# Talking-heads attention and two feed-forward layers on one core: the second head mix with its weights stationary on 64x32 tiles, transposes on VectorE, and attn @ v on 64x64 tiles

## The chip, the cores and the metric

The kernel runs on 1 core of a Trainium2 chip. The metric is the device time of one execution in microseconds (us), the median of several runs; lower is better.

## What is computed

```python
scores = scale * np.matmul(q, k.transpose(0, 1, 3, 2))            # 4 batches, 12 heads, 448 x 448, head size 64
scores = np.einsum('bhij,hg->bgij', scores, w_pre)                # first mix over heads
scores = scores - np.max(scores, axis=-1, keepdims=True)
attn = np.exp(scores)
attn = attn / (np.sum(attn, axis=-1, keepdims=True) + 1e-09)
attn = np.einsum('bhij,hg->bgij', attn, w_post)                   # second mix over heads
x = np.matmul(attn, v)                                            # to 1792 tokens x 768
h = x @ w_in; g = s * np.maximum(h, 0) ** 2 + b; x = g @ w_out    # layer 1, 768 -> 2048 -> 768
h = x @ w_in2; g = h * np.cos(h); out = g @ w_out2                # layer 2
```

All inputs and the output are fp32.

## The kernel before, in words

The first part (`attention`, lines 199 to 481) computes the attention, the second (`mlp`, line 500 on) the two layers. The change touches the attention alone, apart from three tables of numbers that set the order.

**Tiling of the attention.** The 448 query rows of a batch are cut into 4 blocks (`BLOCKS`) of 120 or 110 rows, and a block into tiles of 10 rows (`R`): 45 tiles a batch, 180 in all. Tiles are worked on in pairs, 90 of them. Steps of the program, by the name of the tile that each writes:

- `heads` (line 288) loads q and k of two heads by DMA (`raw`, in batch 0 `at` serves as the room for it), turns them on TensorE (`tk`, `tq`, line 306, 48 steps of 4 transposes) and copies the result out of PSUM to `kt` and `qt`.
- `scores` (line 324) multiplies q and k of two heads for one block, on the two 64-row halves of the array (`sps`, line 336, 96 steps of 2 matmuls of 448 columns). Two copies bring the result out of PSUM into `s`, two DMAs per step (line 352) from there into `m`, in which a partition is a pair of row and head.
- `mix` (line 387) is the first mix, for a pair of tiles: 4 matmuls of 448 columns, on the four 64x64 quarters of the array, into two PSUM tiles `p` (line 393). VectorE takes the row maxima (`rmax`, line 400, `st`), ScalarE the exponentials with their sums (`expo`, line 406, `e`), VectorE adds 1e-9 and inverts (lines 412 and 413), GpSimd multiplies w_post by the inverse sums (`weigh`, line 415, `w`).
- `mixt` (line 421) is the second mix, again for a pair of tiles: 16 matmuls, 4 chunks of 112 keys by 2 halves of a tile's rows by 2 tiles. Here `e` (60 x 112) is the stationary operand and the weights `w` are streamed, 60 columns, so that the result `a` comes out with keys on the partitions:

```python
for c in range(4):
    for y in range(2):
        for z in range(2):
            nc.tensor.matmul(out=ha[z].tile[...][:, c, :, y * G:(y + 1) * G], lhsT=he.tile[64 * z:64 * z + K, y, c * CH:(c + 1) * CH],
                             rhs=hw2.tile[64 * z:64 * z + K, y], start=True, stop=True, tile_position=(64 * z, 0))
```

- `keep` (line 441) copies each `a` (112 x 480) into `at`, on ScalarE or VectorE.
- `prod` at line 458 is attn @ v, once per half batch and 4 heads (24 steps): 16 matmuls `vps` (line 464) of 112 x 64 weights from `v` and 230 or 220 columns from `at`, 2 side by side in the array's columns; 2 copies to `xo`, one DMA to `x` in HBM (line 475).

**What sets the order.** Every step is given to a planner (`Plan`, line 38) with a position (`pos`, a due time), the engines that may do it and a cost on each. `Plan.run` keeps a clock per engine, and lets each engine take the ready step with the smallest position; the program is then emitted in that order, and each engine executes its own instructions in it. A step marked `EV` (the copies out of PSUM) goes to ScalarE or VectorE, whichever the planner finds free. `STEP`, `LEAD`, `OFF`, `PRO`, `VW`, `W1` to `W3`, `AVP`, `AVL`, `TOK`, `WT0` and `TAIL` make the positions.

**Rings.** A step that writes a tile waits until the tile's ring has a free place. In PSUM, 8 banks: `ps` has 2 places (for `tk`, `tq`, `sps` and `vps`; a `sps` step takes both, each of the others one), `pa` 2 (both for one `mixt`), `pp` 4 (two for one `mix`). `at` has 2 places, a half batch each; `m` has 2, a block each.

The `mlp` part loads weights, splits each into two parts on ScalarE, VectorE and GpSimd, and runs `hidden` (`h`, line 704) and `output` (`o`, lines 767 and 797); its first steps are placed among the last ones of the attention.

Of the kernel before, what the change touches and what calls it, by code (L numbers as in the profile page):

```python
# [22 lines left out]
CH = 112  # L23
TOKENS = (512, 512, 256, 512)
# [170 lines left out]
STEP = 2374.9  # L195
# [3 lines left out]
def attention(pl, tc, q, k, v, w_pre, w_post, cst, x, mid, left, right, psl, psr):  # L199
# [6 lines left out]
    NG = H // 2  # L206

# [80 lines left out]
    def heads(what, b, g, p):  # L288
# [4 lines left out]
        def raw(new=False):  # L293
            if b == 0:
                i = g * 8 * D
                return at_all[:CH, int(what == "q")].rearrange("p c h w -> p (c h w)")[:, i:i + 8 * D].rearrange("p (z h d) -> p z h d", h=2, z=4)
# [19 lines left out]
    v_all = v_p.tile([CH, 3, 4, 4, D], F32, name="v")  # L316

    def values(b, c, p):
        hv = vh[b, c] = pl.hold(f"v{c}")
# [4 lines left out]
    def scores(n, g, p):
# [19 lines left out]
        first_e = pl.add(p + 800, EV, (430.0, 535.0), lambda e: evac(e, 0), [a], take=[hs], use=hp[:1])  # L344
        ev = [first_e, pl.add(p + 850, EV, (430.0, 535.0), lambda e: evac(e, 1), [a], use=hp[1:], behind=[first_e])]
# [35 lines left out]
    for i in range(NTL // 2):  # L381
# [13 lines left out]
        a = pl.add(p - OFF[0] * STEP, "pe", 840, mix, [d for n in ms for d in m_done[n]] + [c1, m_zero], take=hp, use=[mh[n] for n in ms])  # L395
# [3 lines left out]
        for y in range(2):  # L399
# [4 lines left out]
            m = pl.add(p - (OFF[1] - .1 * y) * STEP, "dve", 560, rmax, [a] + got[:1], take=[] if y else [hst])  # L404
# [474 lines left out]
```

## Time and profile before

| | us |
|---|---|
| median of 3 runs (1410.46 to 1412.24) | 1411.2 |
| the profiled execution, its own time | 1410.2 |
| its span, first to last instruction | 1408.4 |

The profile is of that one execution; the 1.8 us between its time and its span lie around the instructions. Busy time of an engine over the span: TensorE's matmuls (PE) 98%, its weight loads (PEld) 78%, VectorE (DVE) 78%, ScalarE (ACT) 47%, GpSimd (POOL) 31%. A busy time is the length of all records laid over one another, and the records of matmuls overlap, so that a PE that shows as busy has not always all it could do. The rows that matter follow below, each view with its columns.

### The profile page before, as it was taken

The page shows a single profiled execution, that of the slowest core. Times are in us where ns is not written, and L with a number is a line of the kernel's source. Part 1 is how long each engine was busy: PE and PEld are TensorE (multiplying, and loading weights), DVE is VectorE, ACT ScalarE, POOL GpSimd, SP SyncE. Part 2 cuts the span into 40 slices and gives each one's busy share as a digit, 9 for nine tenths or more (in the row PEclk, how much of TensorE's full clock was granted, in tenths as well). Part 3 has the DMA queues.
Part 4 walks back from the last instruction along what each step waited for, and adds up shares of the span by engine and source line. Part 5 has one row for each costly group of instructions (what it writes and reads, how often), then busy time and mean ns, then how long its engine had stood idle before and what let it go on. Part 6 is the DMA issues. An engine that isn't in the chain of part 4 may idle for free.

```text
span 1408.4 us, 25444 instructions
## 1 busy us (share of the span) xinstructions
PE 1383.4 (98%) x9753; PEld 1103.6 (78%) x9753; DVE 1095.8 (78%) x2052; ACT 665.8 (47%) x1385; POOL 429.7 (31%) x415
## 2 busy tenths in 40 slices
PE   7999999999999899999999999999999999999999
PEld 3466565666666688888888888889999999899998
DVE  3566666576577688889887787898799999998975
ACT  1575465465467454323232232466645545445442
POOL 2010000010012443423333243235554444554531
PEclk6899999999999999999999999999999999999999
DMA  6645456444444422221121212112121111211103
GB/s 132 183 129 146 143 138 156 138 130 140 139 148 141 142 68 68 68 67 58 54 71 34 67 47 65 36 34 68 46 68 46 57 57 45 69 45 57 56 35 123
DMA packets 120605, 123.80 MB, mean 88 GB/s; under 512 B 49476, under 2 KB 108324, under 8 KB 120484
## 3 DMA queue, kind: packets, MB, share of 16 engines
q1 hardware_dynamic: 117880, 120.43, 29.6%
q10 hardware_dynamic: 2604, 1.75, 0.5%
q8 instruction: 77, 1.26, 0.4%
q14 instruction: 44, 0.36, 0.1%
HBM read 72.43 MB, written 11.01 MB: 59 GB/s over the span
## 4 chain that ended last, share of the span: by engine, by line
PE 96%; DVE 1%; DMA 1%; ACT 1%; SPq 0%; issue 0%; POOL 0%; DVEq 0%; POOLq 0%
PE h L704 33%; PE o L797 17%; PE o L767 16%; PE a L427 11%; PE sps L336 7%; PE p L393 6%; PE vps L464 5%; PE tq L306 1%; PE tk L306 1%; DMA m<-s 0%; SPq L229 0%; DMA at<-in_q_dram 0%; DMA m<-x 0%; DVE s L235 0%; DVE x L680 0%
## 5 line engine op out<-in xcount | busy, mean ns | idle before, releaser
L652 POOL TENSOR_TENSOR cm<-ca,wh 128x384 f32<-128x384 f32 x128 | 160.8, 1258 | 363.3 <-ACT wh L646 362.6
L704 PE MATMUL h<-m,wh 128*128 128x512 f32 x672 | 217.0, 392 | 0.0
L704 PE MATMUL h<-x,wh 128*128 128x512 f32 (+1 forms) x768 | 192.0, 341 | 5.2 <-DVE x L680 3.8
L427 PEld LDWEIGHTS a<-w,e 60*112 60x112 f32 x2880 | 153.6, 176 | 50.8 <-issue 29.3
L654 POOL TENSOR_TENSOR wl<-cm,ce 128x384 fp32r<-128x384 f32 x128 | 147.5, 1154 | 93.4 <-DVE ce L650 87.3
L427 PE MATMUL a<-w,e 60*112 60x60 f32 x2880 | 161.6, 261 | 3.7 <-POOL w L417 3.5
L417 POOL TENSOR_TENSOR w<-wq,st 128x120 f32<-128x120 f32 x90 | 35.5, 396 | 396.5 <-DVE st L413 306.9
L704 PEld LDWEIGHTS h<-x,wh 128*128 128x128 f32 x768 | 133.0, 190 | 22.5 <-DVE x L680 4.8
L704 PE MATMUL h<-m,wl 128*128 128x512 f32 x384 | 150.6, 392 | 0.0
L704 PEld LDWEIGHTS h<-m,wh 128*128 128x128 f32 x672 | 125.4, 188 | 25.8 <-issue 0.7
L767 PE MATMUL o<-gl,wh 128*128 128x512 f32 (+1 forms) x384 | 139.6, 364 | 0.0
L767 PE MATMUL o<-gh,wl 128*128 128x512 f32 (+1 forms) x384 | 139.6, 364 | 0.0
L409 ACT ACTIVATE e<-p,st 128x448 f32<-128x448 f32 x180 | 113.2, 630 | 55.4 <-DVE st L403 41.6
L767 PE MATMUL o<-gh,wh 128*128 128x512 f32 (+1 forms) x384 | 139.3, 363 | 0.0
L704 PE MATMUL h<-x,wl 128*128 128x512 f32 (+1 forms) x384 | 130.9, 341 | 0.0
L403 DVE TENSOR_REDUCE st<-p 128x1 f32<-128x448 f32 x180 | 109.5, 618 | 21.7 <-PE p L393 19.4
L336 PE MATMUL sps<-kt,qt 64*110 64x448 f32 (+1 forms) x384 | 109.3, 613 | 6.7 <-DVE s L235 5.3
L797 PE MATMUL o<-wh,gl 128*128 128x384 f32 x448 | 114.3, 335 | 0.0
L797 PE MATMUL o<-wh,gh 128*128 128x384 f32 x448 | 114.2, 335 | 0.0
L797 PE MATMUL o<-wl,gh 128*128 128x384 f32 x448 | 114.2, 335 | 0.0
L744 POOL TENSOR_TENSOR tb<-ta,tb 128x512 f32<-128x512 f32 (+1 forms) x64 | 79.0, 1234 | 114.3 <-ACT tb L742 109.4
L806 DVE TENSOR_TENSOR acc<-acc,o 128x384 f32<-128x384 f32 x196 | 99.7, 545 | 14.3 <-PE o L797 14.2
(86 smaller groups left out, 2616.6 us busy)
## 6 DMA issues: line engine op xcount, KB each, us to landing
m<-s SPq DMA_DIRECT2D x144, 192.5 KB
raw<-in_moe_w_in_dram SPq DMA_DIRECT2D x64, 384.0 KB
raw<-in_moe_w_out_dram SPq DMA_DIRECT2D x64, 384.0 KB
m<-s SPq DMA_DIRECT2D x42, 210.0 KB
v<-in_v_dram SPq DMA_DIRECT2D x12, 448.0 KB
out_dram<-acc SPq DMA_DIRECT2D x13, 384.0 KB
raw<-in_k_dram SPq DMA_DIRECT2D x18, 224.0 KB
raw<-in_q_dram SPq DMA_DIRECT2D x18, 224.0 KB
```

The source lines that it names most:

```text
L336: nc.tensor.matmul(out=hp[z].tile, lhsT=hq.tile[64 * z:64 * z + 64, i0:i0 + rows], rhs=hk.tile[64 * z:64 * z + 64], start=True, stop=True, ...
L393: nc.tensor.matmul(out=hp[y].tile[64 * z:64 * z + 64], lhsT=wp[64 * y:64 * y + (K if y else 64)], rhs=src[64 * y:64 * y + (K if y else 64) ...
L403: nc.vector.tensor_reduce(out=hst.tile[:, 0, y:y + 1], in_=hp[y].tile, axis=AX, op=ALU.max, negate=True)
L409: nc.scalar.activation(out=he.tile[:, y], in_=hp[y].tile, func=AF.Exp, bias=hst.tile[:, 0, y:y + 1], accum_out=hst.tile[:, 1, y:y + 1])
L427: nc.tensor.matmul(out=ha[z].tile.rearrange("p (c g r) -> p c g r", c=4, g=H)[:, c, :, y * G:(y + 1) * G], lhsT=he.tile[64 * z:64 * z + K, ...
L652: a = pl.add(p0 + 6 * dp, "pool", 1050, lambda hm=hm, ha=ha, flat=flat: nc.gpsimd.tensor_tensor(out=hm.tile, in0=ha.tile.bitcast(F32), in1 ...
L654: got.append(pl.add(p0 + 7 * dp, "pool", 1050, lambda hm=hm, he=he, flat=flat: nc.gpsimd.tensor_tensor(out=flat(1), in0=hm.tile, in1=he.ti ...
L704: nc.tensor.matmul(out=hp.tile, lhsT=w, rhs=cols(z_, j, k)[:, 0], start=(k == 0 and y == 0), stop=(k == KD - 1 and y == 2))
L744: a = pl.add(p + 7 * dp, "pool", n * 2.4 + 100, lambda h1=h1, h2=h2: nc.gpsimd.tensor_tensor(out=h2.tile, in0=h1.tile, in1=h2.tile, op=ALU ...
L767: nc.tensor.matmul(out=hp.tile, lhsT=w, rhs=x, start=(c == 0 and y == 0), stop=(c == 1 and y == 2))
L797: nc.tensor.matmul(out=hp[e].tile, lhsT=x, rhs=w[:, e * HD:(e + 1) * HD], start=(c == 0 and y == 0), stop=(c == 1 and y == 2))
L806: got.append(pl.add(p, "dve", 470, lambda e=e, hp=hp, view=view: nc.vector.tensor_tensor(out=view(), in0=view(), in1=hp[e].tile, op=ALU.ad ...
```

## The change

The second mix is turned round. The weights `w` (60 x 32, 30 columns of them weights and 2 zeros) are now the stationary operand, and `e` is streamed, 224 columns: 7 runs of 32 keys, every second run of 32. Each of the 16 matmuls of a pair of tiles sits on one of eight 64x32 tiles of the array (2 in the rows, 4 in the columns), and the result `a` has 4 groups of 32 partitions (two halves of the heads by two runs of keys), with the keys along the free axis, 448 in all per tile. `keep` now is a VectorE transpose of 32x32 squares out of PSUM into `at` (2 per pair, each 128 x 448), and always on VectorE. With keys on 64 partitions and two halves of the heads above one another, attn @ v becomes 28 matmuls on the four 64x64 quarters, 7 steps along the keys, in two PSUM tiles, so that it takes both places of `ps`; each matmul streams runs of 5 elements of `at`, one run every 32. `v` is loaded in 24 DMAs of 64 partitions with pieces of 64 elements, in place of 12 with pieces of 256. The copies out of `vps` are 4 of 110 or 120 elements in place of 2 of 220 or 240, `xo` is written in runs, and `kt` and `qt` too are written in order and read in steps from PSUM. The planner's costs and positions are set anew.

```diff
-    wq = one.tile([128, H, G], F32, name="wq")
+    wq = one.tile([128, 64], F32, name="wq")
...
-            copy(e, ht.tile.rearrange("p (w z) -> p z w", z=4) if what == "q" else ht.tile.rearrange("p (z w) -> p z w", z=4), hp.tile)
-        t_done[what, b, g] = pl.add(p + 600, EV, (430.0, 535.0), evac, [a], use=[hp])
+            copy(e, ht.tile.rearrange("p (w z) -> p w z", z=4), hp.tile.rearrange("p z w -> p w z"))
+        t_done[what, b, g] = pl.add(p + 600, EV, (600.0, 680.0), evac, [a], use=[hp])
...
-    v_all = v_p.tile([CH, 3, 4, 4, D], F32, name="v")
+    v_all = v_p.tile([128, 3, 2 * KB, D], F32, name="v")
...
+        v_done[b, c] = got = []
+        for z in range(2):
+            got.append(dma(p, lambda z=z: v_all[64 * z:64 * z + 64, c], lambda z=z: v[b, GH * z + 2 * c:GH * z + 2 * c + 2].rearrange("h (k p) d -> p (h k) d", p=64),
+                           64 * 2 * KB * D * 4, take=[] if z else [hv], behind=got[:1] + m_done[0][-1:], rate=200.0))
...
-            for c in range(4):
-                for y in range(2):
-                    for z in range(2):
-                        nc.tensor.matmul(out=ha[z].tile.rearrange("p (c g r) -> p c g r", c=4, g=H)[:, c, :, y * G:(y + 1) * G], lhsT=he.tile[64 * z:64 * z + K, y, c * CH:(c + 1) * CH],
-                                         rhs=hw2.tile[64 * z:64 * z + K, y], start=True, stop=True, tile_position=(64 * z, 0))
+                h.tile = ps_a.tile([128, 512], F32, tag="a", name="a")[:, :2 * KB * 32]
+            for y in range(2):
+                for u in range(2):
+                    for c in range(2):
+                        for z in range(2):
+                            o = 64 * u + 32 * c
+                            nc.tensor.matmul(out=ha[z].tile[o:o + 32].rearrange("p (y k w) -> p y k w", y=2, w=32)[:, y], lhsT=hw2.tile[64 * z:64 * z + K, y, 32 * u:32 * u + 32],
+                                             rhs=he.tile[64 * z:64 * z + K, y].rearrange("p (k c w) -> p k c w", c=2, w=32)[:, :, c], start=True, stop=True, tile_position=(64 * z, o))
...
-            def keep(e, h=ha[z], slot=slot, col=col):
-                copy(e, at_all[:CH, slot].rearrange("p c h w -> p (c h) w")[:, :, col:col + R], h.tile.rearrange("p (c r) -> p c r", r=R))
-            kept[half].append(pl.add(p + 1000 + 100 * z, EV, (500.0, 600.0), keep, [a] + kept[half][:1], take=[hb] if new else [], use=ha[z:z + 1]))
+            def keep(h=ha[z], slot=slot, unit=unit):
+                nc.vector.transpose(out=at_all[:, slot].rearrange("p k (u w) -> p u k w", w=32)[:, unit:unit + 2], in_=h.tile.rearrange("p (y k w) -> p y k w", y=2, w=32))
+            kept[half].append(pl.add(p + 1000 + 100 * z, "dve", 640.0, keep, [a] + kept[half][:1], take=[hb] if new else [], use=ha[z:z + 1]))
...
+            hp, ho = [pl.hold("ps"), pl.hold("ps")], pl.hold("xo")
...
+                for k in range(KB):
+                    for y in range(2):
+                        for z in range(2):
+                            w = (2 * pp + y) * G
+                            nc.tensor.matmul(out=hp[z].tile[64 * y:64 * y + 64].rearrange("p (u r) -> p u r", r=G), lhsT=v_all[64 * z:64 * z + 64, pp, y * KB + k],
+                                             rhs=at_all[64 * z:64 * z + 64, hf, k, :n // G * 32].rearrange("p (u w) -> p u w", w=32)[:, :, w:w + G],
+                                             start=(k == 0), stop=(k == KB - 1), tile_position=(64 * z, 64 * y))
...
+                        copy(e, ho.tile[:, z, i0 - base:i0 - base + rows].rearrange("p (r t) -> p r t", r=R), hp[z].tile[:, c0:c0 + rows].rearrange("p (t r) -> p r t", r=R))
...
-STEP = 2374.9
+STEP = 2426.2
...
-MIXT = 1100.0
+MIXT = 860.0
```

The order moves with it. TensorE in the third batch, before (`p` first mix, `a` second mix, `sps` scores, `vps` attn @ v; L427 is `mixt`):

```order
L336 MATMUL sps<-kt,qt 110x448 x2
L393 MATMUL p<-m,wp 64x448 x4
L464 MATMUL vps<-at,v 64x220 x16
L427 MATMUL a<-w_2841,e 112x12x5 x16
L464 MATMUL vps<-at,v 64x220 x16
L427 MATMUL a<-w_2875,e 112x12x5 x16
L393 MATMUL p<-m,wp 64x448 x4
L336 MATMUL sps<-kt,qt 110x448 x2
L427 MATMUL a<-w_2956,e 112x12x5 x16
L393 MATMUL p<-m,wp 64x448 x4
L336 MATMUL sps<-kt,qt 110x448 x2
```

and now, at about the same place (the lines have moved: L435 is `mixt`, L342 the scores, L399 the first mix):

```order
L435 MATMUL a<-e,w_3222 32x224 x16
L342 MATMUL sps<-kt,qt 110x448 x2
L399 MATMUL p<-m,wp 64x448 x4
L342 MATMUL sps<-kt,qt 110x448 x2
L399 MATMUL p<-m,wp 64x448 x4
L342 MATMUL sps<-kt,qt 110x448 x2
L435 MATMUL a<-e,w_3331 32x224 x16
L399 MATMUL p<-m,wp 64x448 x4
L342 MATMUL sps<-kt,qt 110x448 x4
L435 MATMUL a<-e,w_3392 32x224 x16
```

Before, apart from the opening of the program, no two steps of `sps` follow each other directly; now they do in places (`sps ... x4`).

VectorE at the same place, before (`st` the statistics of the softmax, `at` the copies of `keep`, `s` those of the scores):

```order
L235 COPY at<-a 112x48x10
L235 COPY s<-sps 110x448
L403 TENSOR_REDUCE st<-p 128x1
L235 COPY at<-a 112x48x10
L403 TENSOR_REDUCE st<-p 128x1
L235 COPY s<-sps 110x448
L403 TENSOR_REDUCE st<-p 128x1
L412 TENSOR_SCALAR st<-st 128x2
L413 RECIPROCAL st<-st 128x2
L235 COPY s<-sps 110x448
L403 TENSOR_REDUCE st<-p 128x1 x2
```

and now:

```order
L237 COPY s<-sps 110x448
L419 RECIPROCAL st<-st 128x2
L409 TENSOR_REDUCE st<-p 128x1 x2
L237 COPY s<-sps 110x448
L418 TENSOR_SCALAR st<-st 128x2
L450 STREAM_TRANSPOSE at<-a 128x2x7x32 x2
L409 TENSOR_REDUCE st<-p 128x1
L237 COPY s<-sps 110x448
L419 RECIPROCAL st<-st 128x2
L409 TENSOR_REDUCE st<-p 128x1
```

Each pair of tiles now has both of its `keep` steps on VectorE, one behind the other, where one of the two mostly went to ScalarE; fewer copies of `s` stand between them.

TensorE at the end of the attention, before (`h` is the first work of the feed-forward layers):

```order
L427 MATMUL a<-w_5023,e 112x12x5 x16
L393 MATMUL p<-m,wp 64x448 x4
L427 MATMUL a<-w_5059,e 112x12x5 x16
L704 MATMUL h<-m,wh 128x512 x2
L704 MATMUL h<-m,wl 128x512
L704 MATMUL h<-m,wh 128x512 x2
L704 MATMUL h<-m,wl 128x512
L427 MATMUL a<-w_5123,e 112x12x5 x16
L427 MATMUL a<-w_5160,e 112x12x5 x16
L704 MATMUL h<-m,wh 128x512 x2
```

and now:

```order
L435 MATMUL a<-e,w_5297 32x224 x16
L399 MATMUL p<-m,wp 64x448 x4
L435 MATMUL a<-e,w_5307 32x224 x16
L399 MATMUL p<-m,wp 64x448 x4
L435 MATMUL a<-e,w_5385 32x224 x16
L435 MATMUL a<-e,w_5414 32x224 x16
L435 MATMUL a<-e,w_5457 32x224 x16
L435 MATMUL a<-e,w_5483 32x224 x16
L474 MATMUL vps<-at,v 64x220 x56
L717 MATMUL h<-m,wh 128x512 x2
```

The `h` steps that stood among the last second mixes now follow them, and four second mixes stand next to each other.

## Rows read from the trace of the kernel before

**Rows 1.** Chain of waits, by engine and line: shares of the 1408.4 us span.

```profile
by line: PE h L704 32.9%; PE o L797 16.5%; PE o L767 16.4%; PE a L427 10.6%; PE sps L336 6.5%; PE p L393 6.0%; PE vps L464 5.4%; PE tq L306 0.8%; PE tk L306 0.6%; DMA m<-s 0.4%; SPq L229 0.4%; DMA at<-in_q_dram 0.4%; issue 0.4%; DMA m<-x 0.
```

**Rows 2.** Four stretches (us): busy us (instructions) per engine, PEclk, DMA share, GB/s.

```profile
0.00:45.00 45.00, 34.69 (x97) 13.81 (x101) 14.28 (x24) 7.68 (x12) 9.26 (x5) 0.61 0.69 149
45.00:440.00 395.00, 391.68 (x4593) 248.36 (x4585) 261.87 (x584) 230.54 (x553) 35.48 (x88) 1.00 0.51 144
440.00:500.00 60.00, 52.06 (x399) 40.66 (x400) 41.84 (x82) 30.64 (x67) 23.24 (x19) 0.89 0.39 123
500.00:1408.00 908.00, 905.02 (x4673) 800.76 (x4671) 777.84 (x1364) 396.97 (x755) 361.75 (x304) 1.00 0.19 58
```

**Rows 3.** Timeline, 200 to 222 us: start, length, engine, line, operation, tiles [idle before].

```profile
201.26 0.98 PE L393 MATMUL p<-m,wp 64*64 64x448 f32 x8
...
202.17 1.78 PE L427 MATMUL a<-w,e 60*112 60x60 f32 x32
...
203.89 3.33 PE L464 MATMUL vps<-at,v 112*64 112x230 f32 x32
...
207.15 0.60 PE L306 MATMUL tk<-ident,raw 112*128 112x112 f32 x4
...
219.19 0.99 PE L336 MATMUL sps<-kt,qt 64*110 64x448 f32 x4
219.38 0.66 DVE L235 COPY at<-a 112x480 f32<-112x480 f32 x1 [1.14 <-PE a L427]
219.43 0.58 ACT L233 ACTIVATE at<-a 112x480 f32<-112x480 f32 x1 [1.22 <-PE a L427]
220.18 0.62 DVE L235 COPY s<-sps 110x448 f32<-110x448 f32 x1
...
220.86 0.60 PE L306 MATMUL tk<-ident,raw 112*128 112x112 f32 x4 [0.68 <-DVE s L235]
```

**Rows 4.** Groups by line, 45 to 440 us: busy us, mean ns | idle before, releaser.

```profile
L427 PE MATMUL a<-w,e 60*112 60x60 f32 x2720 | 151.2, 259 | 0.9 <-POOL w L417 0.7
L427 PEld LDWEIGHTS a<-w,e 60*112 60x112 f32 x2720 | 143.9, 175 | 45.6 <-issue 27.9 <-POOL w L417 15.3 <-POOL cm L652 0.7
L409 ACT ACTIVATE e<-p,st 128x448 f32<-128x448 f32 x175 | 110.1, 630 | 55.4 <-DVE st L403 41.6 <-DVE st L412 11.8 <-DVE st L413 1.6
L403 DVE TENSOR_REDUCE st<-p 128x1 f32<-128x448 f32 x175 | 106.4, 618 | 21.6 <-PE p L393 19.4 <-POOL w L417 0.6
...
L235 DVE COPY s<-sps 110x448 f32<-110x448 f32 (+1 forms) x93 | 57.4, 622 | 8.2 <-PE sps L336 4.9 <-ACT e L409 0.2
L235 DVE COPY at<-a 112x480 f32<-112x480 f32 x86 | 56.4, 658 | 58.8 <-PE a L427 58.5
...
L235 DVE COPY xo<-vps 128x220 f32<-128x220 f32 (+1 forms) x32 | 17.8, 556 | 26.9 <-PE vps L464 26.3
L233 ACT ACTIVATE qt<-tq 128x448 f32<-128x448 f32 x16 | 15.7, 982 | 20.2 <-PE tq L306 20.2
L412 DVE TENSOR_SCALAR st<-st 128x2 f32<-128x2 f32 x86 | 14.3, 166 | 12.7 <-ACT e L409 12.6
L413 DVE RECIPROCAL st<-st 128x2 f32<-128x2 f32 x86 | 14.0, 162 | 2.1
...
L235 DVE COPY kt<-tk 128x448 f32<-128x448 f32 x12 | 7.5, 622 | 4.3 <-PE tk L306 4.3
```

**Rows 5.** Timeline of the DMA issues on SP, 220.8 to 232 us.

```profile
222.35 0.77 SPq L229 DMA_DIRECT2D m<-s  x1
223.22 0.64 SPq L229 DMA_DIRECT2D raw<-in_k_dram  x1
```

**Rows 6.** Timeline of TensorE, 440 to 470 us.

```profile
447.44 1.78 PE L427 MATMUL a<-w,e 60*112 60x60 f32 x32 [0.57 <-POOL w L417]
451.44 3.24 PE L427 MATMUL a<-w,e 60*112 60x60 f32 x32 [2.21 <-POOL w L417]
```

More of the change, by code (lines that the diff above doesn't have):

```diff
@@ L295, in raw @@
                 i = g * 8 * D
[L296 removed]
+                return at_all[:CH, int(what == "q")].rearrange("p c w -> p (c w)")[:, i:i + 8 * D].rearrange("p (z h d) -> p z h d", h=2, z=4)
             if new:
@@ L352, in scores @@
             m_done[n].append(dma(p + 1300, lambda z=z: place(z), lambda z=z: hs.tile[:rows, z], rows * S * 4, ev[z:z + 1], take=[hm] if g == 0 and z == 0 else [], use=[hs],
-                                 behind=m_done[n][:1], cost=870.0, two=n == 0))
+                                 behind=m_done[n][:1], cost=770.0, two=n == 0))
     for g in range(NG):
@@ L394, in attention @@
         ms = sorted({t["n"] for t in pair})
-        a = pl.add(p - OFF[0] * STEP, "pe", 840, mix, [d for n in ms for d in m_done[n]] + [c1, m_zero], take=hp, use=[mh[n] for n in ms])
+        a = pl.add(p - OFF[0] * STEP, "pe", 920, mix, [d for n in ms for d in m_done[n]] + [c1, m_zero], take=hp, use=[mh[n] for n in ms])
         for n in ms:
@@ L403, in rmax @@
                 nc.vector.tensor_reduce(out=hst.tile[:, 0, y:y + 1], in_=hp[y].tile, axis=AX, op=ALU.max, negate=True)
-            m = pl.add(p - (OFF[1] - .1 * y) * STEP, "dve", 560, rmax, [a] + got[:1], take=[] if y else [hst])
+            m = pl.add(p - (OFF[1] - .1 * y) * STEP, "dve", 620, rmax, [a] + got[:1], take=[] if y else [hst])
             def expo(y=y, hp=hp, he=he, hst=hst):
@@ L456, in attention @@
         for pp in range(H // 4):
-            hp, ho = pl.hold("ps"), pl.hold("xo")
-            def prod(pp=pp, hp=hp, b=b, n=n, hf=hf):
-                hp.tile = ps_s.tile([128, 512], F32, tag="s", name="vps")[:, :2 * n].rearrange("p (g n) -> p g n", g=2)
-                for z in range(2):
-                    for c in range(4):
-                        for y in range(2):
-                            g = 2 * z + y
-                            nc.tensor.matmul(out=hp.tile[64 * y:64 * y + 64, z], lhsT=v_all[:, pp, g, c], rhs=at_all[:CH, hf, c, 4 * pp + g, :n],
-                                             start=(c == 0), stop=(c == 3), tile_position=(0, 64 * y))
@@ L466, in attention @@
-            a = pl.add(p + apart * 2 * pp, "pe", 3300.0, prod, kept[b, hf] + [v_done[b, pp]], take=[hp], use=[hb, vh[b, pp]])
-            def evac(e, hp=hp, ho=ho, blocks=blocks, base=base, wid=wid):
-                ho.tile = xo_p.tile([128, 2 * width[0]], F32, tag="xo", name="xo")[:, :2 * wid].rearrange("p (g n) -> p g n", g=2)
-                c0 = 0
-                for i0, rows in blocks:
-                    copy(e, ho.tile[:, :, i0 - base:i0 - base + rows].rearrange("p g (r t) -> p g t r", r=R), hp.tile[:, :, c0:c0 + rows].rearrange("p g (t r) -> p g t r", r=R))
-                    c0 += rows
@@ L474, in attention, with prod @@
-            a = pl.add(p + apart * (2 * pp + 1) + 500, EV, (740.0, 830.0), evac, [a], take=[ho], use=[hp])
+            hp, ho = [pl.hold("ps"), pl.hold("ps")], pl.hold("xo")
+            def prod(pp=pp, hp=hp, n=n, hf=hf):
+                for h in hp:
+                    h.tile = ps_s.tile([128, 512], F32, tag="s", name="vps")[:, :n]
+                for k in range(KB):
[5 more added lines that the diff above has]
+                                             start=(k == 0), stop=(k == KB - 1), tile_position=(64 * z, 64 * y))
@@ new lines, in attention, with evac @@
+            a = pl.add(p + apart * 2 * pp, "pe", 2880.0, prod, kept[b, hf] + v_done[b, pp], take=hp, use=[hb, vh[b, pp]])
+            got = []
+            for z in range(2):
+                def evac(e, z=z, hp=hp, ho=ho, blocks=blocks, base=base, wid=wid):
+                    if z == 0:
+                        ho.tile = xo_p.tile([128, 2 * width[0]], F32, tag="xo", name="xo")[:, :2 * wid].rearrange("p (g n) -> p g n", g=2)
+                    c0 = 0
+                    for i0, rows in blocks:
+                        copy(e, ho.tile[:, z, i0 - base:i0 - base + rows].rearrange("p (r t) -> p r t", r=R), hp[z].tile[:, c0:c0 + rows].rearrange("p (t r) -> p r t", r=R))
+                        c0 += rows
+                got.append(pl.add(p + apart * (2 * pp + 1) + 500, EV, (420.0, 420.0), evac, [a], take=[] if z else [ho], use=hp[z:z + 1], behind=got))
```

63 lines of the change are left out of this document (32 added, 31 removed).

## The prediction

> **What bounds the kernel now.** I first read the chain of waits by line [rows 1]. Nearly all of it is TensorE: the feed-forward layers, which the change leaves alone (lines 704, 767, 797), and the four kinds of attention work. The reader is to see the shares: the second mix 10.6%, scores 6.5%, first mix 6.0%, attn @ v 5.4% of 1408.4 us. Then the stretches [rows 2]: between 45 and 440 us PE is busy for 391.7 of 395 us at granted clock 1.00, VectorE for 262 (66%), ScalarE for 231 (58%), DMA at half. TensorE's own work sets this stretch, so what is taken from it there is gained, until something else gets in the way. Before 45 us and after 500 us nothing in this change touches what bounds. The timeline [rows 3] gives the price of each step, the groups by line [rows 4] those of the other engines.
>
> **TensorE, the prices.** From the chain: the second mix is 0.106 x 1408.4 = 149 us for 90 steps, 1.66 us each; the first mix 84.5 us, 0.94 each; attn @ v 76 us for 24 steps, 3.17 each. The timeline has the same steps from start to start: 0.91, 1.72 and 3.26 us [rows 3]. The first mix streams 4 x 448 = 1792 columns on four tiles of the array and takes 0.94 us; attn @ v streams 16 x 225 = 3600 on two and takes 3.17. If tiles ran in turn, the first would cost half of the second; it costs under a third. So I count rounds, that is columns of matmuls that sit on different tiles once: 448 for the first mix, 8 x 225 = 1800 for attn @ v. Through these two points: (3.17 - 0.94) / 1352 = 1.65 ns a column, and 0.20 us fixed.
>
> The old second mix has 8 rounds of 60, 480 columns, which would be 0.99 us. It takes 1.66; the other 0.67 us I put to its 32 loads of 112 columns (175 ns a record, [rows 4]), too long to hide behind 60 columns. The **new second mix** has 2 rounds of 224: 448 columns, as many as the first mix, hence 0.94 us. Gain 0.72 x 90 = 65 us. Bounds: it cannot be under 448 x 1.65 = 0.74 (18 us more gain); if its loads, 32 columns in place of 112, were as little hidden as before, it costs 0.67 x 32 / 112 = 0.19 us more (17 us). I take 0.94, since the first mix, with the same columns and loads twice as wide, has that. The **new attn @ v** has 7 rounds of 225 on four tiles: 0.20 + 1575 x 1.65 ns = 2.80 us; gain 0.37 x 24 = 9 us. Together 74 us.
>
> **VectorE.** `keep` is 2 transposes of 448 elements from PSUM per pair. None is in the trace. The nearest rows are a reduction (618 ns) and a copy (622 ns) of the same 448 elements from PSUM; a shorter copy (556 ns) is the lower end, the copy with a stepped write (`qt`, 982 ns) the upper [rows 4]. I take 620. VectorE then has, with the counts of the new order: 180 reductions 111 us, 180 transposes 112, 90 pairs of small steps 30, 76 score copies 47, 19 of the heads 12, 42 of `xo`, shorter than 556 ns, say 13: 325 us. ScalarE loses its 91 copies of 0.58 us [rows 3] and gets more of the scores' ones. The attention past 45 us took about 409 us and should take about 366, so VectorE goes from 66% to 89%. It does not set the end by its sum, but whoever waits for it waits longer.
>
> **What gives part of it back**: waits that the old order did not have.
> - *Two places of `ps`.* A score step fills both and must be copied out: from one to the next user 1.67 us, in which PE waits 0.68 for the copy [rows 3], against 0.95 us of work. Counted over the whole order, two score steps now stand next to each other in 11 places outside the opening (before: none). 116 of the 192 copies go to ScalarE, so at least 20 pairs are copied one after the other: 1.0 us each, 11 us.
> - *Two places of `pa`.* The two copies ran side by side on two engines [rows 3]; now both are VectorE's, one behind the other. From one second mix to the next: 0.94 + 0.1 + 1.24 + 0.1 = 2.4 us. Four stand next to each other at the end (3 x 1.5 = 4 us), and 9 pairs have only a score step between them: 2.4, and 0.4 for what VectorE is in the middle of, against 1.9: 8 us.
> - The other 22 places with one short step between two users of `ps`: 0.2 each, 4 us.
> - *The passage to the layers.* Before, PE waited there too, 0.57 and 2.21 us for the weights of second mixes [rows 6], with 52 of 60 us busy at clock 0.89 [rows 2]. The `h` steps that filled gaps now come after; VectorE, which also prepares the layers' first weights, is fuller: 4 us.
>
> Together 31 us.
>
> **At nothing.** 12 more issues on SP, 0.64 us each for such a load [rows 5]: 8 us on a queue with 186 x 0.77 + 84 x 0.64 = 197 us of work in 366; covered, and needed only a half batch later. GpSimd's 128 in place of 120 elements: it is busy for 35 of 395 us [rows 2]. `qt` should fall from 982 toward the 622 of `kt` [rows 4], some 9 us off ScalarE and VectorE; the copies of `xo` double in number and halve in length. Both lie beside TensorE; without that cover up to 10 us either way.
>
> **Sum**: 1410.2 (the profiled execution) - 74 + 31 = 1367; the median of the runs stands 1.0 us above that execution, so 1368.
>
> **Rivals.**
> - *TensorE stays the only bound.* The planner fills every gap as it does now. For it: 99% busy today. Against: the eleven places, and VectorE at 89%. 1411 - 74 + 5 = 1342. Chance 0.12.
> - *VectorE becomes the bound.* If a transpose costs 982 ns, the upper row, it has 65 us more, 390 in all, and the attention cannot be shorter than that: 409 - 390 = 19 us gained, 4 lost in the passage: 1396. For it: both copies on one engine. Against: the reduction and the copy read PSUM at 0.62. Chance 0.10. [...]
> - *Slower: the eight tiles do not run at once.* The trace shows two column tiles with two row tiles together, never four. If four matmuls run at a time, the second mix has 4 rounds of 224: 0.20 + 896 x 1.65 ns = 1.68 us, what it costs now. Only attn @ v's 9 us are gained, and with TensorE's work as long as before half of the waits are covered: 1411 - 9 + 15 = 1417. This decides from 0.94 + 43 / 90 = 1.42 us per step on. Chance 0.07. That would also be the case in which the change does not do what it says.
> - *Slower: streaming `at` in short runs.* attn @ v reads 5 elements, skips 27. In the rows, steps in memory cost: `qt` 982 ns against 622 [rows 4]. If a column cost twice as much there, a step takes 2.6 us more, 62 us in all, of which waits absorb some: 1411 - 74 + 62 + 16 = 1415. It decides from 2.80 + 43 / 24 = 4.6 us on. Against: `qt` steps at every element, here it is one in five. Chance 0.07. [...] No row of this trace shows TensorE reading in steps.
>
> **How the numbers follow.** My case has 0.64, with its own range 1350 to 1390 (the loads, the transposes, half or one and a half times the waits). The range takes in most of the first rival below and the second above, 1340 to 1400; the two slower ones, 0.14, stay outside. A change of under 0.2%, about 3 us, cannot be told from none here. Faster 0.86: my case and the first two rivals. The last two end near 1416 but could land by the old time: slower 0.11, same 0.03.
>
> **What would show it.** In the profile after: second mix start to start near 0.94 us and its 32 records nearly all overlapping; 1.7 means four at a time. attn @ v at 2.8; over 4.6 means the short runs cost. The transposes' mean near 620 ns and VectorE 85 to 90% busy in the attention; at 98% it is the bound. PE's waits for copies of scores and for transposes near 30 us in all. The layers should keep their 908 us from the first `o` on. If PE shows no waits, the first rival was right; if the loss sits in the first weights of the layers, my 4 us for the passage was too little.

## The result and the profile after

The changed kernel takes 1368.6 us (median of 4 runs, 1364.53 to 1372.31), the kernel before 1410.8 in the same job: ratio 0.970 [0.966, 0.974]. Forecast was 1368, with 1340 to 1400 as the range. The four runs lie in two pairs, near 1365 and near 1372 us, and the median stands between them. The profiled execution took 1364.5 us, its span is 1362.7, against 1410.2 and 1408.4 before: 45.7 us less.

The chain of waits by line, of the kernel after [rows 1]:

```profile
by line: PE h L717 33.8%; PE o L810 17.1%; PE o L780 17.0%; PE sps L342 6.6%; PE a L435 6.2%; PE vps L474 5.3%; PE p L399 5.3%; DMA m<-s 1.6%; PE tk L310 0.9%; issue 0.8%; PE tq L310 0.8%; DVE at L450 0.8%; DVE s L237 0.5%; DMA at<-in_k_dra
```

The second mix fell from 10.6% to 6.2%, and the chain is still TensorE's. New or longer in it are the transposes (DVE `at`, 0.8%), copies of scores (DVE `s`, 0.5%) and the DMAs from `s` to `m` (1.6%, before 0.4%).

Stretches of the kernel after [rows 2], with the same columns:

```profile
0.00:45.00 45.00, 35.76 (x105) 14.91 (x109) 12.94 (x26) 7.27 (x12) 9.26 (x5) 0.60 0.70 149
45.00:395.00 350.00, 334.03 (x5084) 155.78 (x5076) 269.07 (x640) 196.85 (x527) 34.60 (x86) 0.99 0.60 162
395.00:460.00 65.00, 57.02 (x509) 40.99 (x502) 53.40 (x97) 33.03 (x80) 27.62 (x22) 0.87 0.40 126
```

The windows are set so that the second one holds nearly the same work as 45 to 440 us did: 2720 matmul records of the second mix, 85 steps, in both, and two of the 90 first mixes fewer (86 for 88). So 45 us are gained in the attention, and what follows lasts as long as before (968.4 us, now 967.7). VectorE is busy for 269 of 350 us, 77%; PE has 16 us without any matmul in flight, before 3.3.

Groups by line, 45 to 395 us [rows 4]:

```profile
L415 ACT ACTIVATE e<-p,st 128x448 f32<-128x448 f32 x174 | 110.0, 634 | 62.3 <-DVE st L409 43.3 <-PE a L435 10.4 <-DVE st L418 5.8
L409 DVE TENSOR_REDUCE st<-p 128x1 f32<-128x448 f32 x175 | 104.7, 609 | 18.9 <-PE p L399 16.7 <-POOL w L423 0.4 <-issue 0.2
L450 DVE STREAM_TRANSPOSE at<-a 128x448 f32<-128x448 f32 x168 | 99.8, 629 | 22.5 <-PE a L435 21.6
L435 PE MATMUL a<-e,w 60*32 60x224 f32 x2720 | 89.0, 358 | 2.0 <-POOL w L423 0.9 <-DVE at L450 0.9
L235 ACT ACTIVATE s<-sps 110x448 f32<-110x448 f32 (+1 forms) x107 | 55.7, 543 | 47.6 <-PE sps L342 38.0 <-DMA m<-s 6.4 <-issue 1.7
L435 PEld LDWEIGHTS a<-e,w 60*32 60x32 f32 x2720 | 43.1, 106 | 60.6 <-issue 26.9 <-POOL w L423 22.7 <-DVE at L450 4.0
L237 DVE COPY s<-sps 110x448 f32<-110x448 f32 (+1 forms) x67 | 40.9, 615 | 11.3 <-DMA m<-s 5.4 <-PE sps L342 4.1
L235 ACT ACTIVATE qt<-tq 128x448 f32<-128x448 f32 x14 | 7.6, 544 | 5.8 <-PE tq L310 5.8
```

A transpose is 629 ns long, beside a reduction of 609. The loads of the second mix are 106 ns a record (175 before) and 43 us in all (144). `qt` fell from 982 to 544 ns.

Timeline of the kernel after, 170 to 178 us [rows 3]:

```profile
171.13 0.98 PE L399 MATMUL p<-m,wp 64*64 64x448 f32 x8
171.23 0.98 ACT L235 ACTIVATE s<-sps 110x448 f32<-110x448 f32 x2 [1.03 <-PE sps L342]
...
172.04 0.99 PE L435 MATMUL a<-e,w 60*32 60x224 f32 x32
...
172.96 1.01 PE L342 MATMUL sps<-kt,qt 64*110 64x448 f32 x4
173.12 1.18 DVE L450 STREAM_TRANSPOSE at<-a 128x448 f32<-128x448 f32 x2 [0.26 <-PE a L435]
...
173.89 0.13 PEld L435 LDWEIGHTS a<-e,w 60*32 60x32 f32 x2 [0.67 <-issue]
173.91 1.42 PE L435 MATMUL a<-e,w 60*32 60x224 f32 x32
...
174.35 0.56 PEld L435 LDWEIGHTS a<-e,w 60*32 60x32 f32 x30 [0.33 <-DVE at L450]
```

From start to start the first mix takes 0.91 us, the second now 0.92 (172.04 to 172.96), before 1.72 here and 1.62 in the median. Both copies of a score step go to ScalarE, one behind the other, 0.98 us for both. The second mix at 173.91 began two of its 32 records, and had to wait with the other 30 until the second of the two transposes was done: 1.42 us instead of 0.99.

PE's steps from start to start, added up by kind over the whole span (worked out from all matmul records; a wait counts with the step before it, and the last step of all, of 16 us, is left out):

| us | before | after |
|---|---|---|
| second mix `a` | 153.2 | 99.4 |
| scores `sps` | 108.8 | 124.6 |
| first mix `p` | 87.8 | 88.1 |
| attn @ v `vps` | 76.5 | 72.7 |
| `tk`, `tq` | 31.9 | 32.9 |
| layers `h`, `o` | 929.0 | 923.3 |

Second mix and attn @ v give back 58 us, the scores take 16 of it. At the median price without a wait, 90 second mixes would be 90 x 0.92 = 83 us and not 99.

### The profile page after: what moved, and what is told of

It is laid out like the page before. It is cut to its first block, busy times and chain, and to the rows that moved or that the text cites. A ratio compares the mean times of both kernels' runs of the same rounds, so it can differ in the third digit from the quotient of the medians.

```text
span 1362.7 us, 26652 instructions
## 1 busy us (share of the span) xinstructions
PE 1325.5 (97%) x10329; PEld 1007.2 (74%) x10329; DVE 1112.8 (82%) x2121; ACT 631.7 (46%) x1365; POOL 432.3 (32%) x415
## 4 chain that ended last, share of the span: by engine, by line
PE 93%; DMA 2%; DVE 2%; ACT 1%; issue 1%; SPq 0%; POOL 0%; DVEq 0%; POOLq 0%; ACTq 0%
PE h L717 34%; PE o L810 17%; PE o L780 17%; PE sps L342 7%; PE a L435 6%; PE vps L474 5%; PE p L399 5%; DMA m<-s 2%; PE tk L310 1%; PE tq L310 1%; DVE at L450 1%; DVE s L237 1%; DMA at<-in_k_dram 0%; ACT s L235 0%; DMA raw<-in_k_dram 0%
## 5 line engine op out<-in xcount | busy, mean ns | idle before, releaser
L665 POOL TENSOR_TENSOR cm<-ca,wh 128x384 f32<-128x384 f32 x128 | 163.9, 1282 | 360.4 <-ACT wh L659 360.4
L717 PE MATMUL h<-x,wh 128*128 128x256 f32 (+1 forms) x768 | 191.7, 340 | 2.7 <-DVE x L693 1.6
L423 POOL TENSOR_TENSOR w<-wq,st 128x128 f32<-128x128 f32 x90 | 36.5, 407 | 357.9 <-DVE st L419 259.1
L342 PE MATMUL sps<-kt,qt 64*110 64x448 f32 (+1 forms) x384 | 113.9, 628 | 15.3 <-ACT s L235 8.6
L450 DVE STREAM_TRANSPOSE at<-a 128x448 f32<-128x448 f32 x180 | 106.9, 629 | 25.1 <-PE a L435 24.1
L787 DVE TENSOR_TENSOR acc<-acc,o 128x512 f32<-128x512 f32 (+1 forms) x168 | 101.2, 614 | 9.5 <-PE o L780 9.1
```

The source lines that it names most:

```text
L342: nc.tensor.matmul(out=hp[z].tile, lhsT=hq.tile[64 * z:64 * z + 64, i0:i0 + rows], rhs=hk.tile[64 * z:64 * z + 64], start=True, stop=True, ...
L450: nc.vector.transpose(out=at_all[:, slot].rearrange("p k (u w) -> p u k w", w=32)[:, unit:unit + 2], in_=h.tile.rearrange("p (y k w) -> p ...
L665: a = pl.add(p0 + 6 * dp, "pool", 1050, lambda hm=hm, ha=ha, flat=flat: nc.gpsimd.tensor_tensor(out=hm.tile, in0=ha.tile.bitcast(F32), in1 ...
L717: nc.tensor.matmul(out=hp.tile, lhsT=w, rhs=cols(z_, j, k)[:, 0], start=(k == 0 and y == 0), stop=(k == KD - 1 and y == 2))
L787: a = pl.add(p, "dve", n * 1.05 + 66, lambda hp=hp, view=view: nc.vector.tensor_tensor(out=view(), in0=view(), in1=hp.tile, op=ALU.add), [ ...
```

## The experiments

All twelve, in the order of what they answer. Ratios are to the kernel before, run in the same job.

| | us | ratio, 95% interval |
|---|---|---|
| the change | 1368.6 | 0.970 [0.966, 0.974] |
| e1 old arithmetic, new order | 1414.7 | 1.003 [1.002, 1.004] |
| e2 new arithmetic, old order's numbers | 1379.0 | 0.979 [0.977, 0.980] |
| e3 row halves in turn | 1367.5 | 0.971 [0.969, 0.973] |
| e4 attn @ v without short runs | 1364.1 | 0.968 [0.966, 0.970] |
| e5 rings 3, 2, 3 | 1378.0 | 0.977 [0.974, 0.980] |
| e6 four places of `s` | 1380.5 | 0.979 [0.978, 0.981] |
| e7 each transpose twice | 1446.4 | 1.026 [1.024, 1.028] |
| e8 attn @ v, 4 of 7 steps | 1353.2 | 0.961 [0.959, 0.963] |
| e9 no 1e-9 step | 1366.0 | 0.969 [0.967, 0.971] |
| e10 half of the maxima | 1363.5 | 0.966 [0.964, 0.968] |
| e11 second mix twice | 1422.3 | 1.008 [1.006, 1.010] |
| e12 e9 with a refitted order | 1352.9 | 0.959 [0.957, 0.961] |

**The theory**: TensorE still sets the end; the new prices are worth 70 us, and waits for buffers of two places give a third of it back. **Rivals**: the gain is the order's; VectorE is the bound.

### Arithmetic or order: e1 and e2

e1 is the kernel before with the new positions and the new costs of the steps that both kernels share; its second mix is priced at 1660 ns:

```diff
-STEP = 2374.9
+STEP = 2426.2
...
-MIXT = 1100.0
+MIXT = 1660.0
```

e2 is the changed kernel with the old positions and the old costs of the shared steps; its second mix keeps 860:

```diff
-STEP = 2426.2
+STEP = 2374.9
...
-PRO = (13.113, 8281.7)
-VW = (9.908, 13.515)
+PRO = (1283.6, 9149.2)
+VW = (4.582, 16.763)
```

> The old second mix, keep and attn @ v, with the new positions and the new costs of the steps that both kernels share (second mix priced at 1660 ns). My theory (the shorter TensorE steps bring the gain): TensorE's work stays at 409 us, so 1411 within 6 us. Rival (the newly set order brings it): 1368 to 1390, with PE idle or waits gone that the kernel before had.

> The changed kernel with the old positions and the old costs of the shared steps. My theory: the second mix still takes 0.92 us against 1.66, attn @ v 2.9 against 3.17, so most of the gain stays; waits grow as the order does not fit: 1368 to 1385. Rival (the order brings it): 1400 or more.

1414.7 and 1379.0 us, both where the theory had them. Without the arithmetic, the new order costs 4 us; without the new order, the arithmetic still gives 31 of the 42 us. That the order is fitted to the prices is worth the other 11.

### Which matmuls run side by side: e3

```diff
-            for y in range(2):
-                for u in range(2):
-                    for c in range(2):
-                        for z in range(2):
+            for z in range(2):
+                for y in range(2):
+                    for u in range(2):
+                        for c in range(2):
```

Now all 8 matmuls of one half of the array's rows stand ahead of the 8 of the other half.

> The second mix's matmuls in another order: all of one tile's 8 before the other tile's, so that four column tiles of one row half come first. The same work. My theory: if the two row halves still overlap in part, 3 rounds of 224 columns, 0.20 + 672 x 1.65 ns = 1.31 us a step, 35 us more on TensorE, of which waits absorb 10: 1393; if they do not overlap at all, 4 rounds, 1.68 us: 1425. Rival (VectorE sets the end now): TensorE's extra is absorbed, under 1380.

1367.5 us, no different from the change: a miss for both values of the theory. The rival's range holds it, but not for the rival's reason, since hardly any work was added for VectorE to hide. Timeline of e3, TensorE:

```profile
177.62 1.01 PE L435 MATMUL a<-e,w 60*32 60x224 f32 x32
178.57 0.63 PE L342 MATMUL sps<-kt,qt 64*110 64x448 f32 x2
```

A step takes 0.95 us, against 0.92. Short windows early in a step, its line alone (records in flight on PE in brackets, then PEld's; the 16 matmuls of a second mix have 32 records). First the first mix of the kernel before, on four tiles, then the second mix of the change, then that of e3:

```profile
210.36:210.41 0.05, 0.05 (x4) 0.05 (x8) 1.00 1.24 346
```

```profile
105.38:105.41 0.04, 0.04 (x8) 0.04 (x12) 1.00 0.37 66
```

```profile
177.62:177.65 0.03, 0.03 (x4) 0.03 (x4) 1.00 0.15 60
177.65:177.71 0.06, 0.06 (x8) 0.06 (x13) 1.00 0.55 209
177.75:177.80 0.05, 0.05 (x8) 0.05 (x12) 1.00 0.76 287
```

Early in a step on four tiles four records are in flight, in the change's step eight. In e3 four are in flight for 30 ns and from then on eight, although the first eight matmuls in program order all sit in one half of the rows. (The ends of matmuls are modelled, so only the first such windows of a step count: later ones overlap two rounds.) That eight tiles work at once is my reading of these windows and of the 0.92 us, where four at a time would be 1.68 by the prediction's estimate; which half of the rows a record of e3 belongs to, no view shows. At 0.95 us a step, the edit did not make the case it was meant to make (four at a time); the price of that case stays unmeasured.

### Short runs of `at`: e4

The right-hand side of attn @ v reads its 230 or 220 elements one after the other in place of runs of 5 in every 32. Same counts, other values: e4 doesn't compute attn @ v.

```diff
-                                             rhs=at_all[64 * z:64 * z + 64, hf, k, :n // G * 32].rearrange("p (u w) -> p u w", w=32)[:, :, w:w + G],
+                                             rhs=at_all[64 * z:64 * z + 64, hf, k, 20 * w:20 * w + n].rearrange("p (u r) -> p u r", r=G),
```

> attn @ v streams 230 or 220 successive elements of at, in place of runs of 5 in every 32: it multiplies other data than the kernel should, the amount of work is the same. My theory (streaming in short runs costs nothing): attn @ v stays at 2.9 us a step within 0.05 us, total within 4 us of the changed kernel. Rival (short runs cost part of the 0.1 us by which it missed 2.80): 2.80 us or less, and 2 to 5 us off the total.

1364.1 us, 4 us under the change, with intervals that overlap; the steps themselves tell more. Timeline of the change, then of e4:

```profile
102.40 3.03 PE L474 MATMUL vps<-at,v 64*64 64x230 f32 x56
105.36 0.99 PE L435 MATMUL a<-e,w 60*32 60x224 f32 x32
```

```profile
105.63 2.95 PE L474 MATMUL vps<-at,v 64*64 64x230 f32 x56
108.51 0.61 PE L435 MATMUL a<-e,w 60*32 60x224 f32 x16
```

2.96 us from start to start in the change, 2.88 at the same place in e4. Over the first 21 steps, the median with 230 columns is 2.88 against 2.96, that with 220 columns 2.76 against 2.84. So the runs cost 0.08 us a step, 2 us in all: not nothing, which the theory said, and far from the doubling that the prediction weighed.

### Is VectorE the bound: e9, e10, e7

e9 leaves out the addition of 1e-9 (the inverse is taken of the sums themselves); e10 leaves out the second row maximum of each pair (both exponentials take the first one); e7 does each transpose twice. The order is otherwise that of the change.

```diff
-        a = pl.add(p - OFF[3] * STEP, "dve", 170, lambda hst=hst: nc.vector.tensor_scalar(out=hst.tile[:, 2], in0=hst.tile[:, 1], scalar1=1e-9, scalar2=None, op0=ALU.add), got)
-        a = pl.add(p - (OFF[3] - .05) * STEP, "dve", 165, lambda hst=hst: nc.vector.reciprocal(out=hst.tile[:, 3], in_=hst.tile[:, 2]), [a])
+        a = pl.add(p - OFF[3] * STEP, "dve", 170, None, got)
+        a = pl.add(p - (OFF[3] - .05) * STEP, "dve", 165, lambda hst=hst: nc.vector.reciprocal(out=hst.tile[:, 3], in_=hst.tile[:, 1]), [a])
```

```diff
-                nc.vector.tensor_reduce(out=hst.tile[:, 0, y:y + 1], in_=hp[y].tile, axis=AX, op=ALU.max, negate=True)
+                if y == 0:
+                    nc.vector.tensor_reduce(out=hst.tile[:, 0, y:y + 1], in_=hp[y].tile, axis=AX, op=ALU.max, negate=True)
...
-                nc.scalar.activation(out=he.tile[:, y], in_=hp[y].tile, func=AF.Exp, bias=hst.tile[:, 0, y:y + 1], accum_out=hst.tile[:, 1, y:y + 1])
+                nc.scalar.activation(out=he.tile[:, y], in_=hp[y].tile, func=AF.Exp, bias=hst.tile[:, 0, 0:1], accum_out=hst.tile[:, 1, y:y + 1])
```

```diff
                 nc.vector.transpose(out=at_all[:, slot].rearrange("p k (u w) -> p u k w", w=32)[:, unit:unit + 2], in_=h.tile.rearrange("p (y k w) -> p y k w", y=2, w=32))
+                nc.vector.transpose(out=at_all[:, slot].rearrange("p k (u w) -> p u k w", w=32)[:, unit:unit + 2], in_=h.tile.rearrange("p (y k w) -> p y k w", y=2, w=32))
```

> The step that adds 1e-9 to the sums of the softmax is left out and the reciprocal reads the sums directly (the sums are 1 or more, so that fp32 loses the 1e-9 anyway). The order of all other instructions is the same. VectorE has 90 x 0.19 us = 17 us less, and each second mix gets its weights 0.19 us sooner. Theory now (TensorE and VectorE hold the end between them, since 78 of the 95 us that the doubled transposes added came out): half to four fifths of it, 1355 to 1361. Rival (it was the longer way to the weights alone, VectorE's amount does not matter): 1364 to 1369.

> The second of the two row maxima of each pair of tiles is left out; both exponentials take the first one's as their shift. 90 x 0.53 = 48 us less on VectorE, order otherwise the same. Theory (both engines hold the end): 15 to 30 us out, 1339 to 1354, since TensorE takes over as VectorE gets shorter. Rival (VectorE alone): 40 or more, under 1329. Rival (TensorE alone): within 5 us of 1368.

> Every transpose of keep is done twice, one behind the other: 180 more VectorE instructions of 0.53 us start to start, 95 us. My theory (VectorE is close to being the bound but is not it: 269 of 350 us busy): 14 us of slack in places that matter are eaten up and it becomes the bound at about 364 of 350: 1395 to 1425. Rival (VectorE already sets the end): all of it arrives, 1455 or more. Rival (VectorE is free of the path): under 1380.

e9 gives 1366.0 and e10 1363.5 us, both outside the theory's ranges (that both engines hold the end) and inside those of the rivals by which VectorE's amount does not matter. In e10 48 us of VectorE's work are gone (90 reductions at 0.535 us from start to start), and the time falls by 5. VectorE was not the bound. In the other direction much more arrives: e7's 180 added transposes cost 78 us, at 1446.4 between the theory's range and the rival's. The added work is more than the 95 us of the expectation: in the trace a transpose and its repetition start 0.66 us apart and not 0.53, 120 us in all. Groups of VectorE in e7, 45 to 395 us:

```profile
L451 DVE STREAM_TRANSPOSE at<-a 128x448 f32<-128x448 f32 x136 | 88.4, 650 | 4.7
L450 DVE STREAM_TRANSPOSE at<-a 128x448 f32<-128x448 f32 x136 | 85.4, 628 | 22.3 <-PE a L435 20.7
```

The chain of e7 has them for the first time in earnest:

```profile
by line: PE h L718 31.8%; PE o L811 16.1%; PE o L781 16.0%; PE a L435 5.5%; DVE at L450 5.0%; DVE at L451 4.7%; PE sps L342 4.0%; PE vps L475 3.1%; PE p L399 2.9%; issue 2.0%; DVE st L409 1.8%; DVE s L237 1.1%; DMA m<-s 0.6%; ACT e L415 0.6
```

Yet VectorE is busy for only 303 of 350 us (86%) there. The second mixes take 142.6 us from start to start, where the change has 99.4, and TensorE's longest wait in total, 45 to 395 us, is this one (us, times, longest):

```profile
PE a L435 <- DVE at L451: 18.8, 33, 1.2
```

Doing a transpose twice also keeps each place of `pa` filled for longer, by the 0.66 us from one to its repetition. Whether VectorE's load or this longer path from one second mix to the next makes the 78 us, e7 can't tell.

### Is TensorE the bound: e11 and e8

e11 does each second mix twice; e8 leaves out three of the seven steps of attn @ v along the keys.

```diff
-            for y in range(2):
+            for y in (0, 1, 0, 1):
```

```diff
-                for k in range(KB):
+                for k in range(4):
```

> Each second mix is done twice into the same place, order otherwise the same: 90 x 0.75 = 68 us more on TensorE. Theory (both engines hold the end): 35 to 60 us come out, 1403 to 1428. Rival (TensorE alone): 65 or more, 1433. Rival (VectorE alone): under 1385.

> attn @ v does 4 of its 7 steps along the keys; the rest of the keys is left out. TensorE has 3 x 225 x 1.65 ns = 1.1 us less in each of 24 steps, 27 us. My theory (TensorE's work still sets most of the stretch): 20 to 27 us come out, 1341 to 1349. Rival (VectorE or the copies set it): under 8 us, above 1360.

e11: 54 of some 68 us added (90 x 0.75, 448 columns more) come out, 79%; as expected. e8: 15 of the 27 us taken away, a miss between the theory's range and the rival's. By the steps from start to start, attn @ v got 25 us shorter there (72.7 to 47.6), and the second mixes, the scores and the first mixes 10 us longer (312.1 to 322.5). TensorE's work counts in both directions, but a shorter step in part only moves waits to other steps.

### More places: e5 and e6

```diff
-N_PS, N_PA, N_PP = 2, 2, 4
+N_PS, N_PA, N_PP = 3, 2, 3
```

```diff
-N_S = 3
+N_S = 4
```

> The changed kernel with 3 places of ps and 3 of pp in place of 2 and 4. My theory (score steps wait 17 us for the two places of ps): those waits fall by half, 1355 to 1363, unless the first mix then waits for a place of pp, which would show at line 399. Rival (the scores wait for VectorE's or ScalarE's turn, not for a place): within 4 us of the changed kernel.

> The changed kernel with 4 buffers for the copied scores (s) in place of 3. Copies wait for a DMA out of s for 12 us in all in the profile after. If these waits hold up the two places of ps: 3 to 8 us faster, 1360 to 1365; if something else ends last there: within 3 us of the changed kernel.

1378.0 and 1380.5 us, both 10 to 12 slower: misses. The planner makes another order as soon as a ring has another size, and that order has more waits: the sum of the score steps from start to start (after 45 us) is 99.6 us in the change, 108.3 in e5 and 103.5 in e6. They tell nothing of the rings by themselves.

### The order refitted: e12

e9 again, with planner costs set near the distances that the trace shows and positions searched anew for them (copies 440 ns on ScalarE and 535 on VectorE in place of 545 and 625, reduction 535 for 620, transpose 540 for 640, which the trace has at 570, second mix 920 for 860):

```diff
-STEP = 2426.2
+STEP = 2522.89
...
-MIXT = 860.0
-PRO = (13.113, 8281.7)
-VW = (9.908, 13.515)
-OFF = (2.325, 3.19, 0.741, -0.393)
+MIXT = 920.0
+PRO = (878.968, 11747.184)
+VW = (-4.902, 9.213)
+OFF = (3.537, 5.257, 0.934, -0.687)
```

> Only the order changes, and the 1e-9 step is left out as in e9_no_add (1366.0 us). The planner's costs are set to the start-to-start distances that the trace of the changed kernel shows (second mix 0.91 us on TensorE, copies 0.44 and 0.535, reduction 0.535, transpose 0.54), and the positions are searched anew. Theory: the some 30 us for which TensorE waits between 45 and 395 us are mostly a matter of the order (two score copies on ScalarE one behind the other, second mixes that wait for the transposes of the one before): a third to two thirds of them go, 1346 to 1360 us. Rival: two places of ps and pa cost that much in whatever order: 1363 to 1380, and the waits of score steps for copies stay near 30 us in the waits by releaser.

1352.9 us (5 runs, 1349.33 to 1353.89), ratio 0.959 [0.957, 0.961]: 13 us under e9, as the theory had it, with the same work in another order (13 of the copies have moved from ScalarE to VectorE). Waits by engine and releaser, 45 to 395 us, first of the change, then of e12 (us in total, times, longest):

```profile
PEld sps L342 <- ACT s L235: 22.5, 25, 1.8
PEld sps L342 <- ACT e L415: 9.9, 20, 0.7
...
PE sps L342 <- ACT s L235: 8.0, 11, 1.2
```

```profile
PEld sps L342 <- ACT s L235: 15.6, 25, 1.0
...
PEld sps L342 <- ACT e L415: 3.9, 11, 0.4
...
PE sps L342 <- ACT s L235: 1.1, 4, 0.6
```

A wait of PEld counts from its own last load and lies partly under matmuls; a wait of PE is time without any. Both fell. From start to start the scores take 108.6 us over the span, as before the change (108.8), where the change has 124.6. The steps in order say why: after 45 us, of the 87 score steps on PE eleven follow another one directly in the change, in the kernel before and in e12 none does. The end of the attention still has its waits in e12: second mixes, attn @ v and `h` together take 648 us there, and 643 in the change.

## Why the prediction was right, step by step

**TensorE sets the end**: right. e11 and e10 show it, 54 of 68 us added to TensorE against 5 of 48 taken from VectorE; e8, 15 of 27 taken from TensorE, fits less well.

**The price of the second mix**, 0.94 us by counting rounds: right, 0.92 in the median. That loads of 32 columns hide behind 224 is the reason I gave; the rows agree (43 us of loads instead of 144), but no run changes the loads alone. That eight tiles work at once fits the eight records in flight in the windows of the change and of e3, and steps of 0.92 and 0.95 us where four at a time were estimated at 1.68.

**The price of attn @ v**, 2.80 us: 0.1 too low, as a mean of the first 21 steps it takes 2.90. e4 shows most of what is missing: read without short runs it takes 2.82, the middle of 2.88 and 2.76. The rival of short runs had the direction right (with runs of 5 the step is longer); the size is 0.08 us on 2.88, 3%.

**The sum**, by the stretch with equal work: 85 x 0.70 = 60 us for the second mix, 6.5 for attn @ v (67.3 to 60.8 us), so 66; gained were 45, so waits took 21 to 22 (some of it is the clock: PEclk is 0.57 from 128 to 132 us). Foreseen for that stretch were 11 + 4 for `ps` and 8 for `pa`: 23. By kind, `sps` lost 17 (82.3 to 99.6 us) and `a` 5 (140.9 to 86.8, where 60 was due). **The eleven places** were the right count: their score steps last 1.80 us on average, 0.95 without a wait, so 9 us in all for 11 foreseen. The other 76 score steps last 1.05 and lost 8 us, for 4 foreseen. e12, which has no such place, gets nearly all of both back (83.7 us). At `pa` the wait is less than foreseen, 5 for 8.

**The passage and the end**, 4 + 4 us: 3.7 net, and one cause was left out, the clock. TensorE in the change, last second mixes, and an earlier one for comparison:

```profile
399.39 0.99 PE L435 MATMUL a<-e,w 60*32 60x224 f32 x32 [0.67 <-POOL w L423]
401.26 2.18 PE L435 MATMUL a<-e,w 60*32 60x224 f32 x32 [0.88 <-DVE at L450]
404.32 2.18 PE L435 MATMUL a<-e,w 60*32 60x224 f32 x32 [0.87 <-DVE at L450]
407.37 2.18 PE L435 MATMUL a<-e,w 60*32 60x224 f32 x32 [0.87 <-DVE at L450]
410.87 4.99 PE L474 MATMUL vps<-at,v 64*64 64x220 f32 x56 [1.31 <-DVE at L450]
```

```profile
129.38 1.74 PE L435 MATMUL a<-e,w 60*32 60x224 f32 x32
```

Stretches of the change and of the kernel before, with the columns of [rows 2]; PEclk, third from the end, is the granted share of TensorE's full clock:

```profile
129.38:131.12 1.74, 1.74 (x35) 0.72 (x34) 0.56 (x1) 0.55 (x1) 0.14 (x1) 0.50 0.15 49
399.39:400.38 0.99, 0.99 (x32) 0.50 (x32) 0.99 (x3) 0.66 (x3) 0.14 (x1) 1.00 0.47 62
400.50:402.00 1.50, 0.73 (x10) 0.37 (x18) 1.50 (x4) 1.44 (x4) 0.51 (x2) 0.88 1.03 367
402.00:414.00 12.00, 8.95 (x130) 4.45 (x118) 10.09 (x22) 4.83 (x10) 3.76 (x5) 0.50 0.27 93
```

```profile
451.00:457.00 6.00, 5.56 (x38) 4.88 (x38) 4.03 (x11) 3.07 (x8) 1.68 (x3) 0.50 0.01 4
```

The starts of the four in a row (399.39, 401.26, 404.32, 407.37) lie 1.87, 3.06 and 3.05 us apart, 8.0 in all, where I had 3 x 2.4 = 7.2. PE was busy for 0.73 of the 1.5 us from 400.5 us on, then the clock was granted at half from 402 to 414 us; before, it was at half from 451 to 457 us, half as long. At half clock the 32 records of a second mix last 1.74 us (129.38) and at full clock 0.99 (399.39), so by this estimate 0.75 of each of the 3.05 is the clock, and the 2.3 that are left are near the 2.4 foreseen. The five second mixes and three attn @ v in that stretch were cheaper by 5 x 0.70 + 3 x 0.29 = 4.4 us, and `h` gave back 5.6 (476.6 to 471.0 us), since the waits of before went out of its steps, which I had not taken off. The stretch ends only 0.7 us sooner, so waits and clock took 9.3 us of this, for 8 foreseen. From the first `o` on the layers last 911.0 us, before 910.4, as foreseen.

**The total.** By the medians the steps gave 90 x 0.70 + 24 x 0.29 = 70 us where I had 74, and 24 net went back where I had 31. The two errors cancel in part, and the runs lie in pairs 7 us apart, so the agreement of the median to 1 us is luck. The mechanism is not, and most terms came within 4 us.

**VectorE at 89%**: too high, 77%. A transpose has the 620 ns that I took (629), but neighbours on the engine overlap: two transposes take 1.18 us, and the 0.57 us by which the next one follows is what counts. Of this the sum used only the length of two transposes, 1.24; the share was the basis of the second rival. VectorE was not the bound: e10 gives 5 us for 48. What it would be worth to have ScalarE do a part of `keep` is shown by no run here: e7 adds transposes on VectorE, and none gives some to ScalarE.

**The slower rivals**: short runs are excluded by 2.90 us a step, where 4.6 would have decided, and by e4; four tiles at a time by 0.92 us a step.

**At nothing**: `qt` fell further than said on ScalarE, to 544 ns. New and not foreseen is that copies of scores wait for the DMAs that empty `s`: 6.4 us on ScalarE and 5.4 on VectorE. A fourth place (e6) came with another order, so what it costs stays open; e12 has 4.8 and 2.0 us of those waits.

## What to carry to other kernels

Price a matmul step by rounds, the columns that sit on different tiles of the array counted once, and fit two points of the trace; it gave two new steps to 0.02 and 0.1 us. When a step gets shorter, look in the new order for neighbours that share a buffer of few places: each of the eleven such places cost 0.85 us, and another order of the same work gave that back. Where waits grow, look at the granted clock too: at 0.50 a second mix here lasted 1.74 us in place of 0.99. A change of ring sizes under a planner is never one change: compare orders first, then times.

## What the runs showed of the hardware

- With all 8 matmuls of one half of the array's rows ahead of the other half's in program order (e3), eight records were in flight 30 ns after the first, and a step took 0.95 us against 0.92 for the interleaved order.
- Reading 5 elements in every 32 as the moving operand cost TensorE 0.08 us on a step of 2.88 or 2.76 us (e4).
- At a granted clock of 0.50 the 32 records of a second mix on eight tiles lasted 1.74 us, at 1.00 they lasted 0.99 (both in the change).
- Of 48 us of work taken from VectorE, 5 came out as time (e10); of 120 us added to it, 78 did (e7, with VectorE 86% busy). One of the two alone would have given a wrong picture.
